# A second DMA queue for one weight matrix, with a new order of stages, in a fused attention and feed-forward kernel

## The chip, the core and the metric

The kernel runs on one core of a Trainium2 chip. A core has five engines that run side by side, each with its own list of instructions taken in order: TensorE (PE in the profile, its weight loads PEld), VectorE (DVE), ScalarE (ACT), GpSimd (POOL) and SyncE (SP), which here does nothing but issue DMA transfers. Engines wait for each other by semaphores only. Transfers are issued from an engine's queue and carried out by 16 DMA engines. TensorE writes to PSUM, which has 8 banks of 2 KB per partition.

The metric is the device time of one execution in microseconds. The time before is a median of three runs.

## What is computed

Two layers, each of windowed attention and then of a feed-forward network, both with a layer norm ahead and a residual sum behind. In short:

```
x: 2048 tokens x 576, bf16
twice:
    y   = layernorm(x)
    q, k, v = y @ wqkv                     # 32 heads of 18 columns
    s   = q k^T / sqrt(18), kept where 0 <= query - key < 256
    x   = x + softmax(s) v @ wo
    y   = layernorm(x)
    h   = gelu(y @ w1 + b1)                # 4608 columns
    x   = x + h @ w2 + b2
```

Both layers use the same weights.

## The kernel before

The tokens are cut into chunks of 512 (four tiles of 128), four chunks per layer, so eight chunks in all. A chunk goes through these stages, by the names that the priorities use:

- `ln`: layer norm; `q`: projections to q, k and v, one stage per tile
- `ea`, `eb`: scores on TensorE, exponentials on ScalarE, mask on GpSimd, product with v on TensorE (PV), for the first and the last four groups of heads
- `t`: output projection, residual, second layer norm
- `ga`, `gb`: y @ w1 and gelu, for the first and the second half of the 4608 columns
- `ma`, `mb`: the halves of h @ w2 (called mm2)
- a `+` behind a name: the stage's weight loads

The stages of neighbouring chunks overlap: the matmuls of mm2 and the projections fill TensorE while ScalarE works on exponentials. Every piece of work is a task with an engine, the buffers that it reads and writes, an assumed duration and a priority. A planner in the program orders the tasks by these when the program is built. What runs on the chip is the resulting fixed order of each engine, with semaphores for the data:

```python
    def add(self, eng, fn, reads=(), writes=(), dma=None, ring=4, cost=0.1, lat=0.1, prio=0.0, ...):
        stage = self.stage + ("+" if dma in ("w1", "w2", "xr") else "")
        prio += self.nudge.get(stage, 0.0)
        # ... (cut) the planner takes the task that can start first, and of those the one with the lowest prio
```

The two feed-forward matrices don't stay on chip: each chunk reads them again. w1 has three buffers of six column blocks. w2 has one buffer for one half of its rows, in three blocks of six rows of tiles, which are reloaded when mm2 has read them for the last time. Both go through SyncE's queue, and so do the DMA transposes:

```python
    def w1_load(prio, reads=()):
        # ... (cut) three transfers for six column blocks
        dma("sp", w1_sb[:, sl, 0:4 * GW]..., cls="w1", cost=0.55, lat=2.0, move=2.15, desc=512, prio=prio)
        for b in range(2):
            dma("sp", w1_sb[64 * b:64 * b + 64, sl, 4 * GW:]..., cls="w1", cost=0.6, ..., prio=prio)

    def w2_load(hf, prio, gate=False):
        for b in range(NFH // WB):                       # NFH = 18, WB = 6: three transfers
            f0 = hf * NFH + WB * b
            dma("sp", w2_sb[:, WB * b:WB * b + WB, :], B_w2[f0 * P:(f0 + WB) * P, :].rearrange("(w p) d -> p w d", p=P),
                reads=[f"h{WB * b}"] if gate else [], writes=[f"w2s{b}"], cls="w2", ring=NFH // WB, cost=0.55, lat=2.0, move=0.44 * WB,
                desc=128 * WB, prio=prio)

    # transposes, all on SyncE: xn -> xnTa or xnTm, qn -> qT or kT, attq -> attT
        add("sp", lambda e: e.dma_start_transpose(dst[:, :, i * 128:(i + 1) * 128], xn[:, sl, :]), ..., dma="t", ring=8, prio=prio)
        add("sp", lambda e, dst=dst, sl=sl: e.dma_start_transpose(dst, qn[:, sl, :]), ..., dma="t", ring=8, prio=prio)
        add("sp", lambda e, i=i: e.dma_start_transpose(attT[:, :, i * 128:(i + 1) * 128], attq[:, i, :]), ..., dma="t", ring=8, ...)
```

ScalarE's list has a fixed order for exponentials and gelus (`fifo="act"`); a transfer issued from ScalarE has none and is placed by the planner between them.

mm2 reads a w2 block in pieces of six matmuls, for each token tile and each half of the output columns:

```python
    def mm2(k, hf, prio):
        for i in range(nt):                              # four token tiles
            for hh in range(2):
                b = Bank(FILL)                           # one of the PSUM banks 4 to 6
                for f0 in range(0, NFH, 6):
                    # ... (cut) six matmuls of 128x128 by 288 columns that read w2 block f0 // WB
                resid(t, hh, b, prio)                    # VectorE adds the bank to x_res
```

The first chunk has an order of projections of its own. Its queries go through DMA transposes and its keys through TensorE:

```python
    QK0 = {("q", 0): -5.0, ("q", 1): -4.9, ("q", 2): -4.8, ("k", 0): -4.7, ("q", 3): -4.6, ("k", 1): -4.5, ("k", 2): -4.4, ("k", 3): -4.3}
```

The first unit of scores of a chunk reads its queries 0 to 2 and its key 0; the second key 1, key 3 and queries 1 to 3. While TensorE would be idle at the start, the planner may put in matmuls on a zero tile (`warm`).

Of the kernel before, what the change touches and what calls it, by code (L numbers as in the profile page):

```python
# [9 lines left out]
P = 128  # L10
# [30 lines left out]
class Sched:  # L41
# [23 lines left out]
    def add(self, eng, fn, reads=(), writes=(), dma=None, ring=4):  # L65
        waits = {}

        def want(ev):
            c, v, _e = ev
            if waits.get(c, 0) < v:  # L70
                waits[c] = v

        for r in reads:
            lw = self.last_write.get(r)
            if lw is not None and not (eng == "pe" and lw[2] == "pe"):
                want(lw)
        for w in writes:
            for rd in self.readers.get(w, ()):
                if rd[2] != eng or rd[3]:
                    want(rd[:3])  # L80
            lw = self.last_write.get(w)
            if lw is not None and not (eng == "pe" and lw[2] == "pe"):
                want(lw)
        if dma is None:
            assert eng != "sp"
            c = self.cnt[eng]
            amount = 1
        else:
            rg = self.ring(eng, dma, ring)
            c = rg.sems[rg.i % rg.k]  # L90
            rg.i += 1
            amount = 16
            if c.val > 0:
                want((c, c.val, None))
        wl = []
        wd = self.waited[eng]
        for cc, v in waits.items():
            if wd.get(cc, 0) >= v:
                continue
            wd[cc] = v  # L100
            wl.append((cc, v))
        c.val += amount
        own = None if dma is not None else eng
        ev = (c, c.val, own)
        self.steps[eng].append(Step(eng, fn, wl, c, amount))
        for w in writes:
            self.last_write[w] = ev
            self.readers[w] = []
        for r in reads:
            self.readers.setdefault(r, []).append((c, c.val, own, dma is not None))  # L110
        return ev
# [297 lines left out]
def build_kernel(nc, A_x, A_wqkv, A_wo, B_x, B_w1, B_b1, B_w2, B_b2, out):  # L409
    D = 576  # L410
# [3 lines left out]
    DH = 18  # L414
    G = 8
    NT = 2048 // P
    KD = 5
# [16 lines left out]
    WB = 6  # L434
# [7 lines left out]
    PL = Plan(S, 7)  # L442
    add = PL.add


    PL.nudge = {"": -2.02, "q1.0": -2.58, "q1.1": 0.31, "q1.2": 0.87, "ln2": 19.43, "ea1": -34.19, "q2.1": -1.41, "q2.2": -16.29, "t1": -2.99,
                "ln3": 8.39, "ma1": -0.55, "q3.0": 6.61, "q3.1": 7.71, "gb1": -7.81, "mb1": 6.43, "ga2": -27.39, "eb3": -3.74, "q4.0": -19.11,
                "q4.2": 40.34, "q4.3": -13.98, "gb2": -6.31, "ea4": -36.93, "mb2": 1.59, "ga3": 2.14, "eb4": 8.59, "ma3": 51.12, "q5.1": -1.29,
                "q5.3": 5.02, "ln6": -1.24, "ea5": -7.66, "eb5": -4.01, "ma4": 15.72, "ma4+": -1.72, "q6.1": -5.64, "q6.2": -0.55, "q6.3": -1.88,
                "gb4": -8.38, "ea6": -1.49, "mb4": -1.02, "q7.0": -0.55, "q7.1": -3.15, "q7.2": 3.63, "t6": 46.29, "ea7": 8.95, "mb5": 58.73,  # L450
                "ma6": 7.37, "t7": -1.09, "mb6": -2.75, "ga7": -2.55}

    def sb(name, shape, dtype):
        return nc.alloc_sbuf_tensor(name, shape, dtype)
# [3 lines left out]
    w2_sb = sb("w2_sb", [P, NFH, D], BF16)  # L458
# [6 lines left out]
    qn = sb("qn", [P, NQN, H * 32], BF16)  # L465
    vA = sb("vA", [P, VS, H, VW], BF16)
    pT = sb("pT", [P, PS, 4, 512], BF16)
    attq = sb("attq", [P, 4, KD * 128], BF16)
# [59 lines left out]
    def dma(q, out_, in_, reads=(), writes=(), cls="w", ring=8, **kw):  # L528
        n = 2 if cls != "xr" else 4
        for s in out_.shape:  # L530
            n *= s
        kw.setdefault("lat", 2.0)
        kw.setdefault("move", n / 330e3)
        kw.setdefault("desc", n // 1152)
        add(q, lambda e: e.dma_start(out_, in_), reads=reads, writes=writes, dma=cls, ring=ring, **kw)
# [29 lines left out]
                                          channel_multiplier=1), writes=["ident"], cost=0.3, prio=-10)  # L565
    add("pool", lambda e: e.memset(xn[:, :, D:KD * 128], 0.0), writes=[f"xn{i}" for i in range(NXN)], cost=0.4, prio=-10)
    for i in range(NQN):
        add("dve" if i % 3 == 1 else "pool", lambda e, i=i: e.memset(qn[:, i, :].rearrange("p (h e) -> p h e", e=32)[:, :, DH:32], 0.0),
            writes=[f"qn{i}h{h}" for h in range(2)], cost=0.5, prio=-9)
    add("dve", lambda e: e.memset(attq[:, :, D:KD * 128], 0.0), writes=["aqd"], cost=0.25, prio=-8)  # L570
    add("dve", lambda e: e.memset(wqkv[64:128, 4, :], 0.0), writes=["wqC", "wkC", "wvC"], cost=1.0, prio=-8)
    add("dve", lambda e: e.memset(wo_sb[64:128, 4, :], 0.0), writes=["woC"], cost=0.4, prio=-8)
    add("dve", lambda e: e.memset(warm[:, :], 0.0), writes=["warm"], cost=0.2, prio=-30)
# [81 lines left out]
    def w2_load(hf, prio, gate=False):  # L655
        for b in range(NFH // WB):
            f0 = hf * NFH + WB * b
            dma("sp", w2_sb[:, WB * b:WB * b + WB, :], B_w2[f0 * P:(f0 + WB) * P, :].rearrange("(w p) d -> p w d", p=P),
                reads=[f"h{WB * b}"] if gate else [], writes=[f"w2s{b}"], cls="w2", ring=NFH // WB, cost=0.55, lat=2.0, move=0.44 * WB,
                desc=128 * WB, prio=prio)  # L660

# [18 lines left out]
    qn_ctr = [0]  # L680
    qn_at = {}

    QK0 = {("q", 0): -5.0, ("q", 1): -4.9, ("q", 2): -4.8, ("k", 0): -4.7, ("q", 3): -4.6, ("k", 1): -4.5, ("k", 2): -4.4, ("k", 3): -4.3}

    def qkv(k, i, prio0):
        l, t0, nt = CH[k]
        A = l * NT + t0 + i
        for n, w in enumerate("qkv"):
            prio = prio0 + (0.8 if k == 1 and w == "v" else 0.0) if k else QK0.get((w, i), -0.55 + 0.01 * i)
            dest = [f"v{A % VS}h{o}" for o in range(2)] if w == "v" else [f"qn{qn_ctr[0] % NQN}h{o}" for o in range(2)]  # L690
# [264 lines left out]
    for i in range(n0):  # L955
        qkv(0, i, -5)
    dma("pool", b2bc[:, :], bass.AP(tensor=B_b2.tensor, offset=B_b2.offset, ap=[[0, P], [1, D]]), reads=["k3"], writes=["b2"], cls="b", ring=2,
        cost=1.0, prio=-1)
# [29 lines left out]
    for k in range(NK + 1):  # L988
        b = 4 * k
# [13 lines left out]
        if k >= 2:  # L1003
            PL.stage = f"mb{k - 2}"
            mm2(k - 2, 1, b)
            w2_load(0, b + 1)
# [3 lines left out]
        if k == 1:  # L1010
            w2_load(0, 1, True)
# [11 lines left out]
        if k >= 1:  # L1023
            PL.stage = f"ma{k - 1}"
            mm2(k - 1, 0, b + 2)
            w2_load(1, b + 3)
# [27 lines left out]
def bass_interleave_layers__sliding_block__mixer_channel_mlp__prompt_kernel(  # L1054
    nc,
    A_x,
    A_wqkv,
    A_wo,
    B_x,
    B_w1,  # L1060
    B_b1,
    B_w2,
    B_b2,
    out,
):
    build_kernel(nc, A_x, A_wqkv, A_wo, B_x, B_w1, B_b1, B_w2, B_b2, out)
# [28 lines left out]
```

The softmax here doesn't subtract the row's maximum and nothing guards it: scores larger than these inputs give would overflow.

## Time and profile before

| | |
|---|---|
| time, median of three runs | 934.54 us (934.08 to 934.91) |
| span of the profiled execution | 932.9 us |
| mean granted TensorE clock | 0.996 |
| HBM read, written | 91.87 MB, 2.36 MB |
| moved by SyncE's queue (q1) | 119.90 MB |
| moved by ScalarE's queue (q10) | 2.65 MB |
| transfers of w2 blocks | 48 of 864 KB |
| transfers of w1 | 48 of 768 KB and 96 of 48 KB |
| DMA transposes, all on SyncE | 152 |

An engine's busy time is the time in which one of its instructions runs; matmuls are pipelined, so a busy TensorE is not by itself at its peak. DMA issues are shown on the issuing engine's queue (SPq, ACTq) and don't count as busy time. A wait is put down to the event that came last before the waiting instruction started; "issue" means that the profile shows none. The line numbers (L920 for instance) are those of the program: L756 scores, L765 exponential, L786 mask, L803 PV, L670 projections, L879 and L891 the two parts of y @ w1, L894 gelu, L920 mm2, L837 residual, L709 and L696 copies of projections out of PSUM, L535 plain transfers, L634, L728 and L847 transposes.

### The profile page before, as it was taken

Reading aid. Unit: us, or ns where it says so; the run is one execution under the profiler, and the core shown is the slowest. Engines: PE = TensorE matmul, PEld = TensorE weight load, DVE = VectorE, ACT = ScalarE, POOL = GpSimd, SP = SyncE. Lnnn points to the kernel's source line nnn. Section 1 sums busy time; section 2 is a strip of 40 time slices with the busy share of each in tenths; the row PEclk is TensorE's granted clock in tenths of the full one; section 3 lists DMA queues with packets and bytes.
Section 4 is the critical chain, followed back from the end, with each engine's and each line's share of the span. In section 5 each row is a group of like instructions: output and inputs, shape, how many; then the busy total and the mean of one; then the engine's idle time right before and its main releaser. Section 6 shows DMA issues by size and latency. Waiting matters only on the chain. (4 is left out here: it accounts for less than half of the span.)

```text
span 932.9 us, 22409 instructions
## 1 busy us (share of the span) xinstructions
PE 900.9 (97%) x9372; PEld 566.1 (61%) x9408; DVE 319.9 (34%) x799; ACT 598.4 (64%) x721; POOL 372.0 (40%) x504
## 2 busy tenths in 40 slices
PE   8898999999999999999999999999999999999998
PEld 6566464565746747566574656657566664657556
DVE  6657211740218412165220833235222530241001
ACT  4776687576772677664577657756676677852541
POOL 3766453362613535144250733506443363610100
PEclk9999999999999999999999999999999999999999
DMA  7997539944369061947429452494527816084430
GB/s 194 145 235 135 156 106 232 192 118 126 117 121 162 11 201 35 264 99 168 120 36 263 76 163 77 98 252 78 165 70 177 184 47 225 26 211 150 153 115 26
DMA packets 221460, 129.01 MB, mean 138 GB/s; under 512 B 151856, under 2 KB 219184, under 8 KB 221360
## 3 DMA queue, kind: packets, MB, share of 16 engines
q1 hardware_dynamic: 212048, 119.90, 52.5%
q0 software_dynamic: 6880, 5.03, 3.0%
q10 hardware_dynamic: 2432, 2.65, 1.0%
q8 instruction: 74, 1.21, 0.5%
q14 instruction: 26, 0.21, 0.1%
HBM read 91.87 MB, written 2.36 MB: 101 GB/s over the span
## 5 line engine op out<-in xcount | busy, mean ns | idle before, releaser
L765 ACT ACTIVATE pT<-ps 128x1024 bf16<-128x1024 f32 (+2 forms) x384 | 348.7, 970 | 145.6 <-PE ps L756 144.6
L786 POOL TENSOR_SCALAR_AFFINE_SELECT pT<-pT 128x512 bf16<-128x512 bf16 (+1 forms) x368 | 281.9, 789 | 275.9 <-ACT pT L765 260.5
L920 PE MATMUL ps<-w_sb,hT 128*128 128x288 bf16 x2304 | 314.6, 287 | 3.1 <-DVE x_res L837 3.1
L894 ACT ACTIVATE hT<-ps,b1col 128x512 bf16<-128x512 f32 x288 | 198.0, 688 | 156.4 <-PE ps L891 155.7
L891 PE MATMUL ps<-xnTm,w_sb 128*128 128x512 bf16 x1116 | 255.5, 379 | 2.9 <-issue 1.6
L920 PEld LDWEIGHTS ps<-w_sb,hT 128*128 128x128 bf16 x2304 | 212.2, 98 | 73.8 <-issue 17.1
L891 PEld LDWEIGHTS ps<-xnTm,w_sb 128*128 128x128 bf16 x1152 | 108.7, 98 | 137.5 <-issue 17.4
L837 DVE TENSOR_TENSOR x_res<-ps,x_res 128x288 f32<-128x288 f32 x160 | 70.9, 448 | 247.2 <-PE ps L920 227.6
L670 PE MATMUL ps<-wqkv,xnTa 128*128 128x288 bf16 x960 | 136.9, 288 | 6.2 <-DVE qn L709 3.1
L670 PEld LDWEIGHTS ps<-wqkv,xnTa 128*128 128x128 bf16 x960 | 87.1, 98 | 41.4 <-DVE qn L709 6.2
L803 PEld LDWEIGHTS ps<-vA,pT 128*128 128x128 bf16 x2880 | 94.1, 96 | 26.8 <-POOL pT L786 7.9
L803 PE MATMUL ps<-vA,pT 128*128 128x20 bf16 x2880 | 100.0, 172 | 5.1 <-DVE attq L818 2.5
L709 DVE CAST qn<-ps 128x288 bf16<-128x288 f32 x120 | 54.4, 455 | 114.7 <-PE ps L670 114.4
L902 POOL TENSOR_TENSOR x_res<-x_res,b2bc 128x576 f32<-128x576 f32 x32 | 44.9, 1402 | 98.0 <-ACT hT L894 98.0
L756 PE MATMUL ps<-qT,kT 32*128 32x384 bf16 (+2 forms) x1216 | 64.5, 278 | 3.1 <-ACT pT L765 2.1
L813 DVE RECIPROCAL rinv<-ps 128x16 f32<-128x16 f32 x64 | 16.3, 255 | 122.4 <-PE ps L803 121.9
L602 POOL TENSOR_SCALAR vtmp<-mv_all 128x1 f32<-128x1 f32 (+1 forms) x43 | 9.3, 216 | 119.9 <-DVE mv_all L593 118.9
L591 DVE BATCH_NORM_STATS2 st_all<-x_res 128x6 f32<-128x288 f32 x104 | 44.5, 446 | 12.3 <-DMA x_res<-in_A_x_dram 11.2
L670 PE MATMUL ps<-wo_sb,attT 128*128 128x288 bf16 x320 | 44.6, 286 | 2.3 <-DMA attT<-attq 1.4
L879 PE MATMUL ps<-xnTm,w_sb 64*128 64x512 bf16 x288 | 39.5, 377 | 3.0 <-ACT pT L765 2.2
L614 DVE TENSOR_SCALAR xn<-x_res,mv_all,rstd 128x576 bf16<-128x576 f32 x52 | 38.2, 737 | 10.6 <-DMA xnTm<-xn 6.9
L756 PEld LDWEIGHTS ps<-qT,kT 32*128 32x128 bf16 x1216 | 19.5, 92 | 34.4 <-issue 21.1
(43 smaller groups left out, 285.9 us busy)
## 6 DMA issues: line engine op xcount, KB each, us to landing
w_sb<-in_B_w_dram SPq DMA_DIRECT2D x48, 864.0 KB, 6.2
w_sb<-in_B_w_dram SPq DMA_DIRECT2D x48, 768.0 KB, 4.7
w_sb<-in_B_w_dram SPq DMA_DIRECT2D x96, 48.0 KB, 4.4
x_res<-in_A_x_dram POOLq DMA_DIRECT2D x4, 1152.0 KB, 9.4
out_dram<-xn SPq DMA_DIRECT2D x16, 144.0 KB, 1.9
wqkv<-in_A_wqkv_dram ACTq DMA_DIRECT2D x3, 576.0 KB, 7.7
hT<-in_A_x_dram SPq DMA_DIRECT2D x2, 576.0 KB, 5.0
wo_sb<-in_A_wo_dram ACTq DMA_DIRECT2D x1, 576.0 KB, 4.4
```

The costliest lines, as they stand in the source:

```text
L591: add("dve", lambda e, i=i, s=s: e.bn_stats(st_all[:, t, i, :], s[:, t, i * HB:(i + 1) * HB]), reads=res, writes=[f"st{t}_{i}"], cost=0.37 ...
L670: ins = e.matmul(bank(bs[o])[:, 0:HB], lhs(c), rhs(c, o * HB), start=(c == 0), stop=(c == KD - 1))
L709: add("dve", lambda e, b=bs[o], dst=dst: e.tensor_copy(dst, bank(b)[:, 0:HB].rearrange("p (h d) -> p h d", d=DH)), reads=[bs[o]], writes=[ ...
L756: ins = e.matmul(two(bs[j // 2])[:, j % 2, col:col + nq * 128], k_of(T0 + so)[0][32 * j:32 * j + 32, g, :], qs[32 * j:32 * j + 32, g, qo * ...
L765: add("act", lambda e, h2=h2: e.activation(pT[:, sl, 2 * h2:2 * h2 + 2, lo:hi], two(bs[h2])[:, :, lo:hi], ACT.Exp, scale=SCALE), reads=[bs ...
L786: add("pool", lambda e, ap=ap, pat=pat, sgn=sgn, kind=kind: e.affine_select(ap, ap, pattern=pat, compare_op=(ALU.is_ge if kind == "d" else ...
L803: ins = e.matmul(bank(B_O)[:, o:o + VW], pT[:, sl, j, col + qi * 128:col + (qi + 1) * 128], vA[:, (T0 + so) % VS, 4 * g + j, :], start=(fi ...
L837: add("dve", lambda e: e.tensor_tensor(x_res[:, t, sl], bank(b)[:, 0:HB], x_res[:, t, sl], ALU.add), reads=[b], writes=[f"x{t}h{hh}"], cos ...
L891: ins = e.matmul(bank(bk)[:, 0:n], w1_sb[:, sl, col:col + 128], xnTm[:, k % 2, c, 0:n], start=False, stop=(c == 3))
L894: add("act", lambda e, ff=ff, fl=fl, bk=bk: e.activation(hT[:, fl, 0:n], bank(bk)[:, 0:n], ACT.Gelu_apprx_tanh, bias=b1col[:, ff:ff + 1]), ...
L902: add("pool", lambda e, t=t: e.tensor_tensor(x_res[:, t, :], x_res[:, t, :], b2bc[:, :], ALU.add), reads=["b2", f"h{fl}"], writes=X(t), co ...
L920: ins = e.matmul(bank(b)[:, 0:HB], hT[:, fl, i * 128:(i + 1) * 128], w2_sb[:, fl, hh * HB:(hh + 1) * HB], start=(fl == 0), stop=(fl == NFH ...
```

## The change

The three transfers of each w2 half are issued from ScalarE's queue in place of SyncE's, with the same blocks of six; transposes and w1 stay on SyncE. It is meant to keep large weight loads from standing ahead of transposes in one queue. The table of priority offsets is replaced by one that was annealed for this arrangement. The first chunk's order of projections alternates again from the start (query 0, key 0, query 1, query 2, key 1, ...), and three memsets of the start move from VectorE to GpSimd. Matmuls, buffers and sizes of transfers are the same.

```diff
-    PL.nudge = {"": -2.02, "q1.0": -2.58, "q1.1": 0.31, "q1.2": 0.87, "ln2": 19.43, "ea1": -34.19, "q2.1": -1.41, "q2.2": -16.29, "t1": -2.99,
     ... (cut)
+    PL.nudge = {"": 4.8, "ea0": 2.97, "ld0+": 36.14, "q1.0": -0.6, "q1.1": -6.69, "q1.2": 0.54, "ln2": 9.06, "t0": 4.48, "q2.0": 8.2, "q2.1": -0.04,
     ... (cut)
     for i in range(NQN):
-        add("dve" if i % 3 == 1 else "pool", lambda e, i=i: e.memset(qn[:, i, :]...[:, :, DH:32], 0.0),
+        add("pool", lambda e, i=i: e.memset(qn[:, i, :]...[:, :, DH:32], 0.0),
             writes=[f"qn{i}h{h}" for h in range(2)], cost=0.5, prio=-9)
-    add("dve", lambda e: e.memset(attq[:, :, D:KD * 128], 0.0), writes=["aqd"], cost=0.25, prio=-8)
+    add("pool", lambda e: e.memset(attq[:, :, D:KD * 128], 0.0), writes=["aqd"], cost=0.5, prio=-8)
     ... (cut)
     def w2_load(hf, prio, gate=False):
         for b in range(NFH // WB):
             f0 = hf * NFH + WB * b
-            dma("sp", w2_sb[:, WB * b:WB * b + WB, :], B_w2[f0 * P:(f0 + WB) * P, :].rearrange("(w p) d -> p w d", p=P),
+            dma("act", w2_sb[:, WB * b:WB * b + WB, :], B_w2[f0 * P:(f0 + WB) * P, :].rearrange("(w p) d -> p w d", p=P),
     ... (cut)
-    QK0 = {("q", 0): -5.0, ("q", 1): -4.9, ("q", 2): -4.8, ("k", 0): -4.7, ("q", 3): -4.6, ("k", 1): -4.5, ("k", 2): -4.4, ("k", 3): -4.3}
+    QK0 = {("q", 0): -5.0, ("k", 0): -4.9, ("q", 1): -4.8, ("q", 2): -4.7, ("k", 1): -4.6, ("q", 3): -4.5, ("k", 2): -4.4, ("k", 3): -4.3}
```

## The prediction

> **What bounds the kernel now.** I read the busy times of the page first, then the same busy times by stretches of 50 us, then the waits of TensorE, then the DMA queues and single stretches of the timeline.
>
> ```profile
> span 932.9 us, 22409 instructions
> PE 900.9 (97%) x9372; PEld 566.1 (61%) x9408; DVE 319.9 (34%) x799; ACT 598.4 (64%) x721; POOL 372.0 (40%) x504
> ```
>
> TensorE (PE) is busy for 900.9 of 932.9 us, so only 932.9 - 900.9 = 32.0 us of the whole span is time in which it does nothing. A busy PE need not be a fast one, so I checked the rate: near the end 132 matmuls of 288 columns take 16.17 us on the chain, 122.5 ns each, and 24 of 512 columns take 5.29 us, 220 ns each. At these rates the two large groups (2304 and 1152 matmuls) make 282 + 254 us, and 1280 projections of 288 columns at about 125 ns make 160 us. These don't shrink by a change of order or of queue.
>
> Where do the 32 us lie? The stretches say it (columns: length, then busy us of PE, of its weight load, of DVE, ACT and POOL, then granted clock, DMA share, GB/s):
>
> ```profile
> 0.00:50.00 50.00, 42.73 (x487) 29.38 (x488) 31.92 (x89) 30.51 (x44) 26.95 (x48) 0.97 1.00 179
> 50.00:100.00 50.00, 45.25 (x678) 31.78 (x676) 32.61 (x78) 37.48 (x45) 34.90 (x51) 1.00 0.83 165
> 100.00:150.00 50.00, 47.02 (x530) 28.02 (x532) 7.43 (x18) 39.49 (x47) 25.01 (x30) 1.00 0.46 137
> 150.00:200.00 50.00, 47.52 (x489) 28.38 (x489) 23.76 (x65) 32.17 (x39) 20.01 (x31) 0.97 0.87 177
> 650.00:700.00 50.00, 49.49 (x552) 30.45 (x552) 11.32 (x27) 36.16 (x42) 22.46 (x27) 1.00 0.35 111
> ```
>
> The first four stretches leave 7.3 + 4.8 + 3.0 + 2.5 = 17.5 us idle; the other 733 us hold 14.5 us together. In the steady part (650 to 700) PE is idle 1%. Nothing there can be won; something can be lost.
>
> The waits of PE by what ended them (us in total, times, longest):
>
> ```profile
> PE ps L756 <- ACT pT L765: 3.2, 11, 0.4
> PE ps L670 <- DVE qn L709: 3.1, 5, 1.5
> PE ps L920 <- DVE x_res L837: 3.1, 6, 1.6
> ...
> PE ps L670 <- DMA attT<-attq: 1.4, 4, 0.6
> ...
> PE ps L756 <- DMA qT<-qn: 0.3, 1, 0.3
> ```
>
> No line is large, and DMA appears with 1.7 us in all. The weight-load rows of the same view add 2.6 us for attT and 0.6 + 0.4 us for qT and kT; they overlap with PE, so 1.7 to 5.3 us is what waits for transposes cost PE directly. Who fills the queue that the change empties:
>
> ```profile
> w_sb<-in_B_w_dram SPq DMA_DIRECT2D x48, 864.0 KB, 6.2
> w_sb<-in_B_w_dram SPq DMA_DIRECT2D x48, 768.0 KB, 4.7
> ```
>
> and two stretches of the timeline (start, length, what):
>
> ```profile
> 446.43 15.78 SPq L535 DMA_DIRECT2D w_sb<-in_B_w_dram  x9
> 44.62 0.94 ACTq L535 DMA_DIRECT2D wo_sb<-in_A_wo_dram  x2
> ```
>
> The 48 loads of 864 KB are the w2 loads (two halves of three blocks in each of eight chunks). In the steady part nine weight loads in a row took 15.78 us to issue, 1.75 us each; the median over all weight loads of both matrices is 0.60 us. Two loads issued from ScalarE (ACT) took 0.94 us, 0.47 us each.
>
> **What the Trainium skill says.** DMA: Bandwidth & Descriptors, section "Issuing engines are not separate DMA queues", says that loads from SyncE, ScalarE and GpSimd end on the same 16 engines, and that a second issuer saves only issue time. So moving w2 brings no bandwidth; this trace has no second busy queue to test that with (the queue of the ACT loads moved 2.65 MB, that of SyncE 119.9 MB). The same page, "Queues, rings and completion order", says that each DMA engine goes round between the queues packet by packet: a transpose would no longer stand behind all of a w2 load, but it would share the engines with it. No run here shows that yet. [...]
>
> **The change part by part.**
>
> (1) *w2 off the SyncE queue.* SyncE loses 48 issues, 48 x 0.60 = 29 us at the median and up to 48 x 1.75 = 84 us with full rings. SyncE computes nothing, so its time is worth only what transposes gain. Landing of attT is 2.6 / 3.9 / 9.5 us (min / median / max), of kT 3.0 / 3.3 / 17.5, of xnTm 2.6 / 2.9 / 6.7: medians lie within 1.3 us of the minimum, part of it from four transposes in a row. With 1.7 to 5.3 us of PE waits on transposes and weight loads of both kinds in front, I take a gain of 2 us.
>
> (2) *w2 onto ACT's queue.* 48 x 0.60 = 29 us of issue time beside 598 us of busy ACT; ACT has 932.9 - 598.4 = 334 us free. The loads come free when mm2 has read a block for the last time, and mm2 is what fills PE during the exponentials. There two exponentials take 1.94 us and a new pair starts every 2.66 to 3.05 us, so ACT has 0.7 to 1.1 us free per unit. One issue fits; three blocks come free within about 1.5 us (each last use is six matmuls, 0.74 us), and three issues are 1.8 us, some 0.7 to 1.1 us more than one unit's slack. Three buffers of pT and PV two units late absorb most of that. I take a quarter of a us for each of 16 groups, +4 us. If each issue has to wait for PE, ACT, which takes its instructions in order, stands still for that long; the planner places the load where it expects the block to be free, so I leave this to a rival.
>
> (3) *First chunk: keys again after the first query.* The first unit of scores reads queries 0 to 2 and key 0. The queries go through transposes of SyncE (three were issued from 13.84 in 5.10 us), the keys through TensorE. Before, scores start at 19.82 us. With key 0 and its PE transpose in between, query 2 is projected one key later: ten matmuls (1.39 us) and one group of transposes (0.61 us), 2.0 us. Most of that work is only moved, so PE isn't idle for all of it; I take +1.5 us because ACT's chain of the first chunk starts later.
>
> (4) *Memsets to GpSimd.* Two of qn and one of attq leave DVE (0.48 + 0.17 = 0.65 us) for POOL, where four of qn took 1.70 us, 0.43 each. That is about 1.2 us more on POOL. Its last memset ended at 3.22 us and its next work starts at 4.74 us after waiting for DVE, so it fits: 0.
>
> (5) *New stage priorities.* They reorder mm2, projections and feed-forward parts around the exponentials. They can touch only the 14.5 us idle after 200 us and some of the 17.5 before, and can open gaps in stretches that have none. The lists are fitted to a model of durations in the program, not to this trace, so I give them 0 with a spread of 5 to 8 us.
>
> Sum: -2 + 4 + 1.5 + 0 + 0 = +3.5 us; 934.5 + 3.5 = 938.
>
> **The rivals.** *First: transposes were the hidden cause.* Several gaps that the list puts down to DVE (1.6 us before a projection at 84 us, 0.87 us before the output projection at 521.6 us) stand where a transposed tile is also needed. If the relief closes these and the new priorities fit the new queues, 6 to 10 us of the 32 go: 925 to 929. Against it: after 550 us gaps over 0.3 us have all but vanished from PE although w2 loads stand in the same queue. *Second: the issue becomes a wait on ACT.* A w2 load waits for PE's last read, and with a full ring takes 1.75 us. If a third of 48 x 1.75 us lies on the path, that is +28 us: about 962. For it: ACT's order is fixed and nothing behind a waiting load runs. Against it: its own ring then holds nothing but w2, and ACT mostly waits for PE already (155.7 us for the feed-forward, 144.6 us for scores). *Third: two queues collide.* DMA share is 1.0 between 600 and 620 us; a transpose next to a w2 load may get half the engines and take some 5 us in place of 2.6. PE would wait at the output projection, eight times for some 1 to 2 us: about 945 to 950. *Fourth: all is hidden*, and the time stays at 934 to 936, which is nearly as likely as my sum.
>
> **Range and chances.** Downwards 32 us of idle PE is the whole stock, and most of the first 17 us belongs to the start, which part 3 doesn't help; -2% would be 916 us and would need 19 of the 32. So faster by over 2% gets 0.02. Upwards there is no such limit: the second rival, or badly placed priorities, reach 953 and more; 0.10. The rest, 0.88, is within 2%. The 8-in-10 range is 927 to 951, wider above.
>
> **What would show it.** Step 1: landing medians of attT and kT fall towards 2.6 and 3.0 us. Step 2: 48 loads of 864 KB on ACT's queue, issue times of some 0.6 us, idle of ACT ended by mm2 small; PE waits for pT grow by up to 4 us over the 3.2 and their weight-load rows. Step 3: first scores at 21 to 22 us, first stretch idle over 7.3 us. Step 5: PE's busy time stays at 901 within 4 us and the idle goes from 32 to about 35 us, by small differences in many stretches. I am wrong if ACT shows long waits ahead of w2 loads, if landing times of transposes grow, or if the idle of the first 200 us falls well below 17.5 us.

## The result, and the profile after

The changed kernel takes 944.21 us (median of four runs, 943.37 to 944.79), the kernel before 934.72 us beside it: a ratio of 1.0101, with a 95% interval of 1.0083 to 1.0118. That is 9.5 us slower. Measured once more, in a later set of runs, the ratio was 1.0128 (1.0103 to 1.0153).

The page's head after the change:

```profile
span 942.2 us, 22376 instructions
PE 901.1 (96%) x9365; PEld 566.7 (60%) x9404; DVE 316.5 (34%) x796; ACT 598.8 (64%) x721; POOL 372.2 (40%) x507
```

TensorE and ScalarE are as busy as before (901.1 for 900.9 us, 598.8 for 598.4). In this execution all of the loss is idle time of TensorE: 942.2 - 901.1 = 41.1 us in place of 32.0. (A few matmul records are missing in each trace, so a single busy time is good to some us only; the waits below are read at their places.) By stretches, with the columns of the earlier table:

```profile
0.00:50.00 50.00, 43.73 (x485) 30.65 (x486) 29.67 (x85) 30.33 (x44) 27.81 (x50) 0.93 0.95 167
50.00:100.00 50.00, 43.67 (x662) 29.09 (x660) 31.12 (x77) 37.51 (x46) 34.53 (x50) 1.00 1.00 173
100.00:150.00 50.00, 48.89 (x545) 29.51 (x544) 8.62 (x21) 39.47 (x46) 25.44 (x31) 1.00 0.47 139
150.00:200.00 50.00, 44.53 (x415) 27.01 (x419) 22.90 (x64) 27.52 (x34) 15.62 (x26) 0.97 0.79 179
...
600.00:650.00 50.00, 46.15 (x425) 28.38 (x429) 24.82 (x60) 27.30 (x33) 13.61 (x21) 1.00 0.82 169
650.00:700.00 50.00, 49.78 (x550) 30.84 (x550) 9.83 (x23) 37.40 (x44) 22.59 (x28) 1.00 0.37 117
700.00:750.00 50.00, 46.89 (x480) 28.32 (x478) 15.07 (x41) 32.28 (x38) 17.45 (x26) 1.00 0.74 164
750.00:800.00 50.00, 47.06 (x534) 28.39 (x536) 8.95 (x22) 37.85 (x44) 23.52 (x29) 1.00 0.45 129
```

The start is no worse: 12.6 us idle in the first 100, 12.0 before. The stretch 650 to 700 is as dense as it was. The loss is lumped: 5.5 us idle at 150 to 200 (2.5 before), 3.9 at 600 to 650 (0.8 before), 3.1 and 2.9 in the two after 700 (0.7 and 0.7 before). TensorE's waits name it:

```profile
PE ps L670 <- DMA attT<-attq: 4.5, 1, 4.5
PE ps L670 <- DMA xnTa<-xn: 4.3, 3, 2.3
PE ps L756 <- ACT pT L765: 4.0, 14, 0.4
...
PE ps L879 <- DVE vA L696: 3.4, 1, 3.4
...
PE ps L756 <- DMA qT<-qn: 2.4, 1, 2.4
```

Few and long waits, nearly all for transposes. Before, DMA ended waits of 1.7 us in this view; here attT, xnTa and qT make 4.5 + 4.3 + 2.4 = 11.2 us. (One xnTa wait of 2.3 us stands at 33 us, in the start, whose idle time in all hardly changed.) The fourth row looks like VectorE, but the timeline shows a transpose there too (start, length, what, and in brackets the idle time before it and what ended it):

```profile
594.68 0.37 ACTq L535 DMA_DIRECT2D w_sb<-in_B_w_dram  x1
597.32 0.97 ACTq L535 DMA_DIRECT2D w_sb<-in_B_w_dram  x2
597.34 5.75 SPq L728 DMA_TRANSPOSE kT<-qn  x2
...
606.62 0.82 DVE L709 CAST qn<-ps 128x288 bf16<-128x288 f32 x2 [4.47 <-DMA kT<-qn]
607.36 0.45 DVE L696 CAST vA<-ps 128x288 bf16<-128x288 f32 x1
...
608.07 0.82 PE L879 MATMUL ps<-xnTm,w_sb 64*128 64x512 bf16 x6 [3.35 <-DVE vA L696]
```

One w2 load leaves ScalarE's queue 2.7 us before SyncE issues two kT transposes, and two more leave in the same moment. The transposes land late, so the qn buffer that they read is not free, the next copy out of PSUM waits 4.47 us, and with it the PSUM bank that the next feed-forward matmuls need.

The queues show that the change did what it says, and what an issue costs ScalarE (ns, min / median / max):

```profile
q1 hardware_dynamic: 174416, 77.43, 38.0%
q10 hardware_dynamic: 40064, 45.13, 15.3%
```

```profile
L535 ACTq DMA_DIRECT2D w_sb<-in_B_w_dram x48: 369/375/1287, 104.6 to 903.8; - x48
```

### The profile page after: what moved, and what is told of

Its sections match the earlier page's. It is cut to its first block, busy times and chain, and to the rows that moved or that the text cites. A ratio compares the mean times of both kernels' runs of the same rounds, so it can differ in the third digit from the quotient of the medians.

```text
span 942.2 us, 22376 instructions
## 1 busy us (share of the span) xinstructions
PE 901.1 (96%) x9365; PEld 566.7 (60%) x9404; DVE 316.5 (34%) x796; ACT 598.8 (64%) x721; POOL 372.2 (40%) x507
## 4 chain that ended last, share of the span: by engine, by line
PE 82%; DMA 7%; DVE 4%; ACT 2%; issue 2%; POOL 1%; SPq 0%; DVEq 0%; POOLq 0%
PE ps L920 27%; PE ps L891 26%; PE ps L670 13%; PE ps L803 6%; PE ps L756 5%; PE ps L879 4%; ACT pT L765 2%; DMA attT<-attq 2%; DMA xnTa<-xn 2%; DVE xn L614 1%; DMA xnTm<-xn 1%; DMA kT<-qn 1%; POOL pT L786 1%; DMA x_res<-qn 1%; DVE x_res L837 1%
## 5 line engine op out<-in xcount | busy, mean ns | idle before, releaser
L891 PE MATMUL ps<-xnTm,w_sb 128*128 128x512 bf16 x1113 | 258.6, 380 | 3.7 <-issue 2.4
L670 PE MATMUL ps<-wqkv,xnTa 128*128 128x288 bf16 x960 | 139.7, 289 | 8.4 <-DMA xnTa<-xn 4.3
L803 PEld LDWEIGHTS ps<-vA,pT 128*128 128x128 bf16 x2880 | 94.7, 96 | 26.8 <-POOL pT L786 11.7
L670 PEld LDWEIGHTS ps<-wo_sb,attT 128*128 128x128 bf16 x320 | 30.6, 99 | 18.7 <-DMA attT<-attq 5.0
```

The costliest lines, as they stand in the source:

```text
L670: ins = e.matmul(bank(bs[o])[:, 0:HB], lhs(c), rhs(c, o * HB), start=(c == 0), stop=(c == KD - 1))
L803: ins = e.matmul(bank(B_O)[:, o:o + VW], pT[:, sl, j, col + qi * 128:col + (qi + 1) * 128], vA[:, (T0 + so) % VS, 4 * g + j, :], start=(fi ...
L891: ins = e.matmul(bank(bk)[:, 0:n], w1_sb[:, sl, col:col + 128], xnTm[:, k % 2, c, 0:n], start=False, stop=(c == 3))
```

## The experiments

Two things differ between the kernels: the queue, and the planned order with the planned moment of each transfer. Planning anew after each edit mixes them. So most of these kernels take a finished plan and change only the queue or the moment of the w2 loads; the order of matmuls, copies and activations then stays exactly the same. (The exceptions are named: two kernels are planned anew, and in two a few tasks are moved.) Three ways of reading the loss stood against each other: the queue, the order of the stages, and, formed after the first runs, the moment of w2 loads relative to transposes.

| run | ratio to the kernel before | 95% interval |
|---|---|---|
| changed order, w2 on SyncE | 1.0060 | 1.0043 to 1.0077 |
| old order, w2 on ScalarE | 1.0019 | 1.0004 to 1.0034 |
| kernel before, new priorities alone | 1.0429 | 1.0411 to 1.0448 |
| changed kernel, old start | 1.0620 | 1.0588 to 1.0653 |
| changed order, no w2 reloads | 0.9984 | 0.9970 to 0.9999 |
| changed order, two places mended | 1.0111 | 1.0082 to 1.0140 |
| the same, w2 on SyncE | 1.0068 | 1.0046 to 1.0089 |
| changed order, w2 later, on ScalarE | 0.9992 | 0.9980 to 1.0004 |
| changed order, w2 later, on SyncE | 1.0020 | 1.0002 to 1.0038 |
| old order, w2 later, on SyncE | 1.0091 | 1.0075 to 1.0107 |
| old order, w2 just ahead of transposes, on ScalarE | 1.0018 | 1.0007 to 1.0029 |
| changed kernel again | 1.0128 | 1.0103 to 1.0153 |

**1. The queue alone, in both orders.**

```diff
-                self.S.add(t.eng, t.fn, ...)
+                self.S.add(self.emit.get(t.dma, t.eng), t.fn, ...)   # emit = {"w2": "sp"} in the changed kernel, {"w2": "act"} in the kernel before
```

> The planned order of the changed kernel on TensorE, VectorE and GpSimd, and that of ScalarE but for the loads; only the 48 w2 loads are put back on SyncE's queue, at the moment that was planned for them. If the queue causes the loss (w2 loads on ScalarE take the DMA engines from transposes that a shared queue would have protected, or hold up ScalarE), the time falls to about 935. If the order of the stages causes it, it stays at 942 to 946, and TensorE still waits about 4.5 us for attT near 161 us.

> The converse: the planned order of the kernel before on all computing engines, with only the 48 w2 loads moved to ScalarE's queue at their planned moment. Queue theory: 942 or more, since the loss comes along with the queue. Order theory: 934 to 937, idle time of TensorE 32 to 35 us.

Moved back to SyncE, the changed order runs at 1.006 with the attT wait still there (4.1 us); moved to ScalarE, the old order runs at 1.0019. So the queue itself is a small part, 0.2% in the old order and 0.4 to 0.7% in the changed one, and the larger part stays with the plan. Neither theory had all of it. Near 160 us the queue made no difference: with w2 on SyncE the first attT took 11.1 us from issue to landing, and 11.5 us in the changed kernel.

**2. The new priorities, and the old start, planned anew.**

```diff
-    PL.nudge = {"": -2.02, ...}          # in the kernel before
+    PL.nudge = {"": 4.8, ...}
```

> The kernel before with the new table of priority offsets alone, planned anew with w2 on SyncE. Order theory: most of the loss, 940 to 946. Queue theory: 934 to 937. Since the table was fitted to the other queue, a time above 946 would say that the two belong together.

```diff
-    QK0 = {("q", 0): -5.0, ("k", 0): -4.9, ("q", 1): -4.8, ...}          # in the changed kernel, with the three memsets back on VectorE
+    QK0 = {("q", 0): -5.0, ("q", 1): -4.9, ("q", 2): -4.8, ...}
```

> The changed kernel with the start of the kernel before (three queries ahead of the first key, three memsets back on VectorE). If the start costs the 1.5 us that the prediction gave it, 942 to 943; if it costs nothing, 944. The new plan also moves later stages, so a difference of a few us in either direction that lies after 100 us is not due to the start.

They take 976.3 and 993.9 us. The first is past 946, the sign that was named for table and queue belonging together, though by far more than the loss to be explained; the second is a miss. The second's loss is not where its edit is. With the old start, the four stretches of 50 us up to 200 are idle 6.8, 7.1, 4.7 and 11.2 us, and those of 500 to 600 and 600 to 700 another 11.7 and 9.8. TensorE's waits with the new priorities alone:

```profile
PE ps L756 <- ACT pT L765: 13.4, 25, 1.4
PE ps L670 <- DMA xnTa<-xn: 7.2, 4, 3.9
```

The first row was 3.2 us in the kernel before: TensorE waits for exponentials at more places (25 for 11), without other matmuls to fill the time. Both edits made the planner start over and gave another plan. Such runs say nothing about the edit itself, so all later runs keep the plan.

**3. Without the w2 reloads.** Of the 48 loads only the first three are issued; mm2 then reads old weights.

```diff
+    for st, t in order:
+        if t.dma == "w2" and t.stage != "ga0+":
+            del at[id(t)]                 # not issued
```

> The changed kernel with the same planned order of every computing engine and of SyncE, but only the first three w2 loads are issued; the other 45 are left out, so mm2 reads old weights and the output isn't the reference's. This takes 38.9 MB off the DMA engines and the loads off ScalarE. If w2 traffic beside the transposes makes them late, the gaps of TensorE at 606 us (3.4), 308 us (1.3) and 161 us (4.5) shrink or vanish, and the time is 933 to 937. If the order alone is at fault, all three stay and the time stays above 941.

The time falls to 0.9984, in the unchanged order of every computing engine. So this order loses nothing by itself: it loses by the w2 loads.

**4. Two places mended.**

```diff
+    for n, i in enumerate((836, 838, 840)):                            # feed-forward tasks, four matmuls each
+        at[id(by[i])] = at[id(by[764])] - 0.03 + 0.01 * n              # ahead of the first output projection
+    for n, i in enumerate((3146, 3147, 3148, 3162, 3163, 3164)):       # w1 transfers
+        at[id(by[i])] = at[id(by[3054])] + 0.01 * (n + 1)              # behind the transpose of the last query
```

> The changed kernel with w2 on ScalarE, and two places of its planned order mended: three feed-forward tasks of four matmuls (2.6 us in all) go ahead of the first output projection near 160 us, and the transpose of the last query goes ahead of six w1 transfers near 740 us. Order theory: the gap of 4.5 us falls to about 2 and that of 2.4 us at 750 us vanishes, so the time falls by 4 to 5 us to a ratio of about 1.005. Queue theory: transposes stay late elsewhere, no more than 2 us are won.

> The same two mends, with w2 back on SyncE's queue at the planned moments. If order and queue add up, the ratio to the kernel before is that of the earlier run with this queue (1.006) less 4 to 5 us, that is about 1.001; together with the run with w2 on ScalarE it says what the queue costs in a mended order: 2 to 4 us if the late transposes of the queue remain.

A miss: the ratios are those without the mends (1.0111 and 1.0068). The first mend worked in its place, the wait for attT fell from 4.5 to 1.8 us; the second didn't: the late qT is gone, but at 752 us TensorE waits 1.9 us for VectorE instead. What was won was lost at other places, which the table under 5 shows.

**5. The same w2 loads, 9 us later.** Of the loads behind the first half of mm2, the 22 that have time (used over 18 us after their planned issue) are issued 9 us later; all 48 stay on ScalarE.

```diff
+    for st, t in order:
+        if t.dma == "w2" and t.stage[:2] == "ma" and first(t) - st > 18:
+            at[id(t)] = st + 9.0
```

> The changed kernel with the w2 loads still on ScalarE, but those that follow the first half of mm2 are issued 9 us later than planned, behind the transposes that stand next to them (they are used 19 us or more after their planned issue). If traffic beside transposes is the queue's cost, the gap at 606 us (3.4) falls below 1 and the one at 161 us shrinks, the time falls by 3 to 6 us. If the cost is ScalarE's time to issue, nothing changes.

This one edit takes the whole loss away: 0.9992 (0.9980 to 1.0004), no different from the kernel before. The place of the earlier timeline, in this run:

```profile
591.02 3.91 SPq L728 DMA_TRANSPOSE kT<-qn  x2
596.72 3.99 SPq L728 DMA_TRANSPOSE qT<-qn  x2
596.73 0.37 ACTq L535 DMA_DIRECT2D w_sb<-in_B_w_dram  x1
```

The first load now leaves 5.7 us after the two kT transposes. Their time from issue to landing (min / median / max of the two), first in the changed kernel, then here:

```profile
DMA to landing us min/median/max: 9.2/9.2/9.2
```

```profile
DMA to landing us min/median/max: 4.4/4.5/4.6
```

With w2 on SyncE at its old moment (run 1) they took 4.4 and 4.5 us as well: there the second and third load stood behind the two transposes. And near 160 us TensorE waits far less for its first attT, which lands 7.5 us after its issue at 152.77 us and not 11.5:

```profile
157.05 2.76 PE L891 MATMUL ps<-xnTm,w_sb 128*128 128x512 bf16 x12
160.29 1.40 PE L670 MATMUL ps<-wo_sb,attT 128*128 128x288 bf16 x10 [0.48 <-DMA attT<-attq]
161.53 1.03 PE L891 MATMUL ps<-xnTm,w_sb 128*128 128x512 bf16 x4
163.41 1.40 PE L670 MATMUL ps<-wo_sb,attT 128*128 128x288 bf16 x10 [0.86 <-DMA attT<-attq]
```

The other three attT are no faster than in the changed kernel (8.9 to 10.9 us for 3.9 to 8.4): the w2 loads now leave while these are under way, but TensorE has other matmuls for most of that time. In the changed kernel, the same matmuls:

```profile
158.13 2.76 PE L891 MATMUL ps<-xnTm,w_sb 128*128 128x512 bf16 x11
165.38 2.11 PE L670 MATMUL ps<-wo_sb,attT 128*128 128x288 bf16 x10 [4.49 <-DMA attT<-attq]
```

Since ScalarE's activations have the same order in these kernels, their start times can be set against each other. The table gives the start of one activation in the changed kernel, and how much earlier (-) or later (+) the same one starts in the runs:

| start in the changed kernel, us | w2 on SyncE | no reloads | mended | w2 9 us later |
|---|---|---|---|---|
| 149.2 | -0.1 | +2.5 | +1.4 | -1.1 |
| 186.5 | +0.2 | -3.8 | -1.8 | -5.7 |
| 306.6 | +0.2 | -3.8 | -1.8 | -5.5 |
| 324.0 | -1.4 | -5.4 | -1.8 | -5.4 |
| 598.2 | -2.0 | -5.0 | -2.3 | -6.3 |
| 617.7 | -3.8 | -8.0 | -0.3 | -9.1 |
| 737.1 | -3.9 | -8.1 | -0.5 | -8.4 |
| 772.6 | -2.6 | -10.3 | +0.6 | -10.5 |

The loss is made up at four places: near 160 us (4.6 us won by the delay, 6.3 without reloads, 3.2 by the mend), near 310 (1.6, by the queue and without reloads, not by the delay), near 608 (2.8 and 3.0) and near 750 (2.1 and 2.2). Loads of w2 are under way beside the late transposes at the first and the third place only. Near 750 the late query stands behind six w1 transfers in its own queue, and ScalarE's queue moves nothing from 738 us on; SyncE's transposes had stood beside w2 loads earlier, from 715 us, where a qT took 9.8 us, and that this made SyncE late is likely but not shown. Near 310 nothing of w2 moves either (no packet of ScalarE's queue from 303 to 309 us), and yet one xnTa takes 4.5 us with w2 on ScalarE, delayed or not, and 2.6 with w2 on SyncE or not reloaded; why, no run shows.

The mended kernel lost 2.0 us at 608, where its order is not changed. Its two kT transposes took 9.7 and 9.3 us, TensorE waited 3.9 us in place of 3.35, and after that the granted clock was lower: 0.66 from 605 to 610 us, where the changed kernel had 1.00. In the start it lost 1.4 us, near 750 another 1.1.

**6. Does the delay help on SyncE, and in the kernel before?** The same edit in two more kernels, a converse one, and the changed kernel once more.

> The changed kernel's planned order, the w2 loads after the first half of mm2 9 us later, and all w2 loads on SyncE. It has both of what helped: later moments, and one queue. If the queue itself costs 0.2 to 0.4% (as the two runs that moved only the queue say), the ratio to the kernel before is 0.995 to 0.998, below that with ScalarE's queue (0.9992), and the gap at 308 us closes. If only the moment counts, it equals 0.999.

> The kernel before with the same delay of 9 us for its 23 w2 loads after the first half of mm2, still on SyncE. Its plan already keeps most w2 loads clear of the output projection's transposes, so I expect a ratio of 0.998 to 1.001. A gain over 0.5% would say that the kernel before too was losing time to its w2 loads.

```diff
+        if t.dma == "w2" and t.stage[:2] == "ma":
+            # just ahead of the chunk's attT transposes, or else of the next transpose; only within 12 us
+            to = aT.get(str(int(t.stage[2]) + 1), 0.0) - 0.3 + ...
+            if not st < to < st + 12:
+                to = min((a for a, x in order if x.dma == "t" and a > st + 1), default=0.0) - 0.3 + ...
+            if st < to < st + 12 and first(t) - to > 8:
+                at[id(t)] = to
```

> The converse: the kernel before in its planned order, w2 on ScalarE, and 19 of its w2 loads moved 0.3 to 8.1 us later, so that they are planned just ahead of the next transposes. The run with the same queue at the old moments gave 1.0019. If the moment beside transposes is what costs, landings of attT, kT and qT grow and the ratio rises to 1.005 to 1.015. If the rest of the changed order was needed for the loss, it stays at 1.002.

> The changed kernel once more, on the chip of the three runs beside it, so that their ratios can be set against it. 1.008 to 1.012 by the first measurement, whatever the theory.

The first three missed, and they set the limits of the explanation. **In the kernel before the delay costs 0.9%.** Its plan had issued three w2 loads at 372.82 us, 3.7 us ahead of the next key's transpose. Delayed, they stand in the same queue right ahead of a query's and a key's transpose, which then take 4.31 and 2.76 us to issue. SyncE falls behind, and six w1 transfers (the x6 below), which had begun to leave at 392.75 us, crowd into the 4.4 us ahead of attT. The waits in brackets are idle time of TensorE:

```profile
380.35 3.00 SPq L535 DMA_DIRECT2D w_sb<-in_B_w_dram  x3
383.39 4.31 SPq L728 DMA_TRANSPOSE qT<-qn  x1
...
397.11 4.41 SPq L535 DMA_DIRECT2D w_sb<-in_B_w_dram  x6
...
401.61 7.41 SPq L847 DMA_TRANSPOSE attT<-attq  x4
...
408.53 1.38 PE L670 MATMUL ps<-wo_sb,attT 128*128 128x288 bf16 x5 [2.05 <-DMA attT<-attq]
```

```profile
749.80 0.61 PE L756 MATMUL ps<-qT,kT 32*128 32x256 bf16 x8 [2.16 <-DMA kT<-qn]
```

In the kernel before the first of these waits was 0.33 us, and the second did not occur. So a loss of the same size comes in the old order, on one queue, by the moment of the loads alone. Of the 9.4 us in its trace 5.0 are idle time of TensorE (37.0 for 32.0); for the rest TensorE is busy longer (905.3 for 900.9 us), at a mean clock of 0.991 in place of 0.996.

**On SyncE, the delay in the changed order** brings 1.0020 in place of 0.9992 (two of its 22 executions, of 1031 and 1733 us, were in a slow state and are left out). The execution whose trace was kept took 942.6 us, above the middle of a spread of 932.7 to 945.1: it wins at 160 and 608 us, then loses 3.7 us between 618 and 700, and near 745 a query's transpose is late by 3.3 us.

**The converse run** cost nothing more (1.0018, and 1.0019 with the old moments on that queue). But it hardly made the collision that it was to make: the median of attT's landing rose from 3.9 to 4.4 us and TensorE's waits for it from 1.6 to 2.6 us, while kT (3.3 for 3.4) and qT (3.8 for 3.7) stayed. So that the moment alone brings the loss on ScalarE's queue in the old order is not shown. No version that issues all its loads clearly beat both kernels: 0.9992 includes 1.

## Why the prediction was right, and where its steps were wrong

938 us was predicted, 927 to 951 as a range; 944.2 lies inside, 6 us above the sum. It owes that to the spread allowed for step 5: none of the three terms that made up the sum was found at its size. The bound was read rightly for the trace that was compared: TensorE's busy time did not change, its idle time did. It need not hold: in the second measurement of the changed kernel, with a span of 951.5 us, TensorE was busy for 907.4 us at a mean clock of 0.986. The terms of the sum fared differently.

**Step 1, -2 us for transposes freed of w2: wrong in sign.** Landing medians were to fall towards 2.6 and 3.0 us. They are 3.7 for attT (3.9 before), and 2.7 for xnTm (2.9), but 3.5 for kT (3.3), 4.1 for qT (3.3) and 3.2 for xnTa (2.6). Growing landing times were one of the prediction's own signs of being wrong. Near 597 us two w2 loads that stood behind two kT transposes in one queue left them at 4.4 and 4.5 us; issued in the same moment from the other queue, they did not. The trace now agrees with what the prediction took from the Trainium skill, DMA: Bandwidth & Descriptors, "Queues, rings and completion order": two kT transposes beside three w2 loads of the other queue took 9.2 us and not 4.4, and the two queues moved packets one for one (last section).

**Step 2, +4 us for ScalarE: not found.** The issue took 0.375 us at the median, not 0.60, ScalarE's busy time is the same, and the run with later loads leaves all 48 issues on ScalarE at 0.9992. Steps 1 and 2 together were put at +2 us; the run that moves only the queue in the old order measured +0.19%, 1.8 us. That the sum fits is luck, since ScalarE's term was not found. Nor does that run show late transposes as the cost: TensorE's idle time is 32.3 us in its trace (32.0 before), and the span grows by busy time at a slightly lower clock (0.994 for 0.996). In the changed order the queue's share does lie at late transposes: with w2 back on SyncE 1.6 us are won near 310 and 1.8 near 608.

**Step 3, +1.5 us for the start: not found.** First scores were expected at 21 to 22 us; they came at 19.2 us, earlier than before (19.8), and the first 100 us are idle 0.6 us more. **Step 4 was right:** GpSimd's last memset ended at 4.31 us, ahead of its next work at 4.63.

**Step 5, the new priorities at 0 with a spread of 5 to 8 us: the term that was mis-sized.** It is what the queue alone leaves: 9.5 - 1.8 = 7.7 us by the old order, 5.6 us (1.0060) by the changed one. The step failed in its path: new priorities were expected to open small gaps in many stretches, and they set the w2 loads at moments that make transposes late. That is the third rival, the collision of w2 loads with transposes, which the prediction tied to the queue and put at the output projection eight times for 1 to 2 us. It came at an output projection once, for 4.5 us, and at a key's transpose, and through the moment of the loads more than through the queue. Near 160 us TensorE had matmuls to do for 160.89 - 153.85 = 7.0 us after the issue of the first attT transpose; this needed 165.38 - 153.85 = 11.5 us, with three w2 loads and two of the x loads (1152 KB each) issued within the 9 us before. The x loads are there in every run; without w2 reloads the first attT took 5.7 us. The kernel before had its attT nearly as late there (up to 9.5 us), but TensorE ran feed-forward matmuls without a gap from the issue at 156.06 us to the projection at 167.97, 11.9 us. The prediction could have asked, for each transpose on the path, what TensorE has to do until it lands.

What stays open: which of the new offsets set the moments; why one xnTa near 310 us is late only with w2 on ScalarE; how far the late queries near 750 go back to w2 loads; and why the queue's own effect changes its sign: ScalarE's queue costs 0.2% in the old order and 0.4% or more in the changed one, but once the loads are later it is SyncE's that costs 0.3% (intervals that nearly touch).

## What to carry to other kernels

A large prefetch has slack and a small transfer that the next matmul needs has none: issue the prefetch behind it, and check in the timeline what stands beside each transfer that ends a wait, rather than only which queue it is in. No fixed delay does this: 9 us took the loss away in one order and cost 0.9% in the other. Cover counts as much as latency: near 160 us a late attT took 10.9 us in the run with later loads and TensorE did not wait for it. To test a scheduler's parts, keep its finished plan and change one thing in that; planning anew turned two edits into +4% and +6%.

## What the runs showed of the hardware that was not expected

**The queues took turns by packets, whatever their size.** What the changed kernel's queues moved (packets, MB, share of 16 engines) from 160 to 161 us, while the late attT are under way beside w2 loads (q10) and x loads from GpSimd (q0):

```profile
q0 software_dynamic: 98, 0.23, 64.9%
q10 hardware_dynamic: 102, 0.12, 32.2%
q1 hardware_dynamic: 99, 0.03, 31.6%
```

from 604 to 606 us, while the late kT are under way beside w2 loads:

```profile
q10 hardware_dynamic: 521, 0.59, 83.0%
q1 hardware_dynamic: 547, 0.13, 30.0%
```

and from 607 to 608 us, with transposes alone:

```profile
q1 hardware_dynamic: 1124, 0.28, 127.6%
```

In each of the first two stretches every queue moves about the same number of packets. A packet of a transpose is small, 0.13 MB in 547 packets, some 0.24 KB; one of a w2 load has 1.1 KB, one of an x load 2.3 KB. So by bytes the transposes got a fifth or less, and in packets 99 and some 270 per us in place of 1124. In the second measurement of the same kernel q10 and q1 moved 729 and 734 packets from 604 to 607 us.

**A gap can lower the clock, but its length does not decide it.** After the 4.5 us gap of the changed kernel TensorE runs slower for a while. The stretches around it (columns as above; the clock is the third from the end):

```profile
160.00:165.00 5.00, 0.89 (x5) 0.20 (x2) 0.00 (x0) 1.37 (x2) 0.00 (x0) 1.00 1.33 315
165.00:170.00 5.00, 4.62 (x21) 2.66 (x22) 2.08 (x6) 0.69 (x1) 0.74 (x2) 0.66 1.05 259
```

Where the delayed loads cut the longest gap to 0.9 us the clock stayed at 1.00; after a gap of 6.6 us in the run with the old start it was 0.50. But the kernel before had 0.50 from 182.5 to 185 us, right after a wait of 1.63 us, so that both kernels have a mean of 0.97 from 150 to 200 us. And the gap near 608 us, 3.35 us in the changed kernel and 3.36 in its second measurement, left the clock at 1.00 in one and brought it to 0.50 in the other:

```profile
610.00:615.00 5.00, 5.00 (x38) 2.74 (x35) 1.63 (x4) 2.67 (x5) 0.00 (x0) 1.00 1.01 136
```

```profile
610.00:615.00 5.00, 4.67 (x30) 2.14 (x29) 0.71 (x2) 1.24 (x2) 0.00 (x0) 0.50 0.68 133
```

The second measurement's trace is 9.3 us longer than the first's with the same order and queue: TensorE is idle 44.1 us in place of 41.1, and busy 907.4 in place of 901.1. So a gap may cost more than its length, the idle time alone doesn't show it, and times of one kernel differ by it. What decides when the clock falls is not shown.
